# Two leftover transposes move into unused slots of the probability turns, with blocks 1 and 2 of q exchanged and a new turn order

## The chip, the core and the metric

The kernel runs on one core of a Trainium2 chip. The metric is device time in microseconds (us) for one execution. Engines: TensorE (PE in the profile; its weight loads are PEld), VectorE (DVE), ScalarE (ACT), GpSimd (POOL) and SyncE (SP, which here only issues DMAs). Each engine works through its own instructions in order and waits on semaphores for the others.

## The reference

Blocked causal attention over 8 batches of 8 heads with 576 positions of 64 values, and then a mixture of 8 experts over the 4608 tokens, each expert taking at most `capacity` = 80 of them:

```python
scores = scale * q @ k.T                       # per batch and head
mask = (pos[:, None] // 64) >= (pos[None, :] // 64)   # by blocks of 64
attn = softmax(where(mask, scores, -1e9))      # sum + 1e-9 below
x = (attn @ v)                                 # tokens x 512
...
expert = argmax(x @ w_gate); gate = softmax(x @ w_gate)[expert]
out[top 80 tokens of e] = gate * (relu(x @ w1[e]) @ w2[e])   # others 0
```

A position sees all positions of its own block and of the blocks before it. There are 9 blocks, so block 0 of q sees one block of k and block 8 sees nine.

## The kernel before

Two heads of a batch make a pair; there are 32 pairs, four to a batch. Attention is a loop over turns, one for each pair, and in a turn each engine works on several pairs at once. The table `TURN` sets the order: each entry names how many pairs ahead or behind of the current one it works on, and what it does, and every engine takes its instructions in the order of the table. `FIRST` and `LAST` are the tables of the turn ahead of the loop and of the last pair; `TURN` runs for 31 turns.

**Scores.** `prep` transposes q and k of a pair (`T0` and `T1`, on VectorE) and scales q (on POOL, into `qt`). `scores` multiplies them in three groups, each with two PSUM banks (one for each head): group 2 (banks 4, 5) holds the tile "56" (blocks 5 and 6 of q on 128 partitions, 448 columns of k) and "08" (block 0 against block 0 of k, block 8 against block 8); group 1 (banks 2, 3) holds "78" with 512 columns; group 3 (banks 6, 7) holds "34" with 320 columns and "12" with 192. `mask` adds a product of two constants that pushes the masked block down. `max` takes the row maximum on VectorE, `merge` joins the two parts of block 8 and block 0, and `soft` is the exponential on ScalarE, which writes the probabilities to `Pt` and their sums.

**Turning.** The probabilities have q on partitions, and the product with v needs k there. `back` transposes them on TensorE, 64 rows by 128 columns at a time: bank pair A for "78" (banks 6, 7), B for "56" (banks 2, 3), C for "34", half of "08" and part of "12" (banks 0, 1), 16 transposes each, and L (bank 0 again) for what is left, block 8's own block and the third block of "12", 4 transposes. `take` copies a bank from PSUM to `PT`: B0 by VectorE, the others by ScalarE (`TAKE`), L with 256 columns and the others with 512. The last slot of each head in B's first bank turns only zeros, because block 5 of q sees six blocks of k, three column tiles, and has nothing in the fourth.

**Values.** `values` multiplies `PT` with v: 14 products, with long runs of neighbouring blocks as one product, into bank 1 (blocks 1 to 8 of q) and a piece of bank 0 (block 0). The last 64 rows of v (`vt`) stand on partitions 0 to 63, with zeros below. `take` V0 (ScalarE) and V1 (VectorE) copy the result to `xT` in the next turn; `flip` transposes it for storing.

**The small steps.** An entry "t" of the table runs one step of the gate's work of a finished batch on VectorE (`recip`, `products`, `shift`, `first_of`, `weight`, `placed`), "pe" its products on TensorE (`logits` in one turn, `logits2` in the next), "ta" its exponential on ScalarE. A batch's steps are spread over four turns.

After attention the kernel picks 80 tokens for each expert and runs the experts' products, bound by TensorE to the end.

## Time and profile before

| | |
|---|---|
| median of 3 runs | 415.36 us (415.18 to 415.41) |
| profiled execution | 412.34 us, span from the first to the last instruction 410.6 us |
| busy in the span | PE 384.8, PEld 243.8, DVE 282.0, ACT 301.3, POOL 125.5 us |
| granted TensorE clock | 0.987 of full speed in the mean |

Attention takes the span's first 290 us or so, the choice of tokens some 18 us, the experts the rest. A busy PE is not PE at its peak: a record begins when an instruction begins to read and ends when its last result is out, so records overlap, and the distance from one start to the next tells what an instruction costs. The same holds for ACT and DVE, to a smaller degree.

### The profile page before, as it was taken

The page shows a single profiled execution, that of the slowest core. Times are in us where ns is not written, and L with a number is a line of the kernel's source. Part 1 is how long each engine was busy: PE and PEld are TensorE (multiplying, and loading weights), DVE is VectorE, ACT ScalarE, POOL GpSimd, SP SyncE. Part 2 cuts the span into 40 slices and gives each one's busy share as a digit, 9 for nine tenths or more (in the row PEclk, how much of TensorE's full clock was granted, in tenths as well). Part 3 has the DMA queues.
Part 4 walks back from the last instruction along what each step waited for, and adds up shares of the span by engine and source line. Part 5 has one row for each costly group of instructions (what it writes and reads, how often), then busy time and mean ns, then how long its engine had stood idle before and what let it go on. Part 6 is the DMA issues. An engine that isn't in the chain of part 4 may idle for free. (4 is left out here: it accounts for less than half of the span.)

```text
span 410.6 us, 13923 instructions
## 1 busy us (share of the span) xinstructions
PE 384.8 (94%) x5383; PEld 243.8 (59%) x5383; DVE 282.0 (69%) x790; ACT 301.3 (73%) x952; POOL 125.5 (31%) x221
## 2 busy tenths in 40 slices
PE   5889999999999999999999999999899999999970
PEld 3556666666666666566666656665578845667530
DVE  5868788997999899899889989998844400100010
ACT  1889999999999999999999999998121222333240
POOL 6324333433335234244433532300147000000010
PEclk9999999999999999999999999999998999999996
DMA  9979999999999999799999899997659999999100
GB/s 125 136 129 200 154 196 129 211 202 160 175 192 172 147 184 169 123 172 190 149 172 182 139 138 288 379 352 210 223 121 270 367 397 398 397 398 378 51 18 20
DMA packets 199287, 84.31 MB, mean 205 GB/s; under 512 B 163677, under 2 KB 182109, under 8 KB 199216
## 3 DMA queue, kind: packets, MB, share of 16 engines
q1 hardware_dynamic: 190320, 65.79, 72.7%
q0 software_dynamic: 6528, 17.28, 15.8%
q8 instruction: 44, 0.72, 0.8%
q10 hardware_dynamic: 2368, 0.30, 0.6%
q14 instruction: 27, 0.22, 0.2%
HBM read 63.21 MB, written 20.33 MB: 203 GB/s over the span
## 5 line engine op out<-in xcount | busy, mean ns | idle before, releaser
L569 ACT ACTIVATE P<-bank,negm 128x192 f32<-128x192 f32 (+2 forms) x320 | 163.1, 597 | 6.8 <-DVE negm L558 5.9
L537 PE MATMUL bank<-T,qt 64*128 64x320 f32 (+3 forms) x512 | 105.0, 502 | 2.0 <-DVE sameE L284 0.6
L558 DVE TENSOR_REDUCE negm<-bank 128x1 f32<-128x192 f32 (+1 forms) x192 | 87.6, 472 | 16.0 <-PE bank L534 15.9
L627 ACT COPY PT<-bank 128x512 f32<-128x512 f32 (+1 forms) x190 | 91.2, 599 | 6.4 <-PE bank L596 6.3
L616 PE MATMUL bank<-PT,vn 128*64 128x384 f32 (+5 forms) x768 | 93.8, 384 | 0.9 <-ACT PT L627 0.9
L569 ACT ACTIVATION_READ_ACCUMULATOR P<-bank,negm 128x1 f32 x320 | 90.6, 286 | 0.0
L596 PEld LDWEIGHTS bank<-ident,P 64*128 64x128 f32 x1664 | 62.7, 138 | 23.7 <-ACT PT L627 18.5
L596 PE MATMUL bank<-ident,P 64*128 64x64 f32 x1664 | 70.5, 226 | 1.7 <-DVE xT L627 0.9
L616 PEld LDWEIGHTS bank<-PT,vn 128*64 128x64 f32 x768 | 47.6, 137 | 40.8 <-issue 31.2
L512 POOL TENSOR_SCALAR qt<-T 128x576 f32<-128x576 f32 x32 | 21.2, 662 | 147.2 <-DVE raw L558 144.7
L537 PEld LDWEIGHTS bank<-T,qt 64*128 64x128 f32 x512 | 43.5, 186 | 16.9 <-issue 4.5
L507 DVE STREAM_TRANSPOSE T<-ld 128x576 f32<-128x576 f32 x64 | 49.1, 768 | 3.2 <-DMA ld<-in_q_dram 3.2
L558 DVE TENSOR_REDUCE raw<-bank 128x1 f32<-128x64 f32 (+1 forms) x128 | 48.7, 437 | 1.6 <-PE bank L537 1.6
L500 POOL DMA_DIRECT2D vn<-in_v_dram x58 | 45.9, 795 | 1.8 <-PE bank L548 0.9
L1001 PE MATMUL ps<-xsT,w 128*64 128x80 f32 x1024 | 40.8, 239 | 1.3 <-issue 1.3
L1001 PEld LDWEIGHTS ps<-xsT,w 128*64 128x64 f32 x1024 | 38.4, 142 | 5.0 <-issue 4.2
L1055 DVE SCALAR_TENSOR_TENSOR y<-av,comb,yt 80x512 f32<-80x512 f32 x7 | 5.2, 746 | 51.6 <-ACT yt L1054 51.6
L1051 PE MATMUL av<-w,hT 128*32 128x512 f32 (+1 forms) x280 | 37.5, 594 | 0.0
L1054 ACT ACTIVATE yt<-ps,gfar 32x512 f32<-32x512 f32 (+1 forms) x18 | 11.4, 635 | 30.1 <-PE ps L1051 30.0
L1060 POOL DMA_INDIRECT out_dram<-y,si x8 | 7.4, 926 | 76.4 <-DVE y L1055 76.4
L1051 PE MATMUL ps<-w,hT 128*32 128x512 f32 (+1 forms) x72 | 29.1, 547 | 0.0
L1021 ACT ACTIVATE hT<-ps 128x320 f32<-128x320 f32 x16 | 7.0, 438 | 26.2 <-PE ps L1001 26.2
(173 smaller groups left out, 373.2 us busy)
## 6 DMA issues: line engine op xcount, KB each, us to landing
w<-in_moe_w_dram SPq DMA_DIRECT2D x13, 2048.0 KB, 20.2
ld<-in_q_dram SPq DMA_DIRECT2D x128, 72.0 KB, 4.1
xs<-Y SPq DMA_DIRECT2D x32, 288.0 KB, 5.4
out_dram<-zero SPq DMA_DIRECT2D x18, 512.0 KB, 6.8
ld<-in_k_dram SPq DMA_DIRECT2D x124, 72.0 KB, 4.0
vn<-in_v_dram POOLq DMA_DIRECT2D x58, 128.0 KB, 4.2
w<-in_moe_w_dram POOLq DMA_DIRECT2D x8, 512.0 KB, 6.4
w<-in_moe_w_dram POOLq DMA_DIRECT2D x8, 256.0 KB, 6.2
```

What stands on the lines that cost most here:

```text
L500: eng.dma_start(self.vn[:, h], v[b, h0 + h, 0:512].rearrange("(j p) d -> p j d", p=P))
L507: nc.vector.transpose(t, self.nat[x].rearrange("p g d -> p (g d)"))
L512: nc.gpsimd.tensor_scalar(q_, t, scalar1=SCALE, scalar2=1.0, op0=ALU.mult, op1=ALU.mult)
L537: nc.tensor.matmul(s[h][:, c:c + n], lhsT=q_[:, P * t - BLK:P * t + BLK], rhs=k_[:, 0:n], start=(c == 0), stop=(g == "1"))
L558: nc.vector.tensor_reduce(to[:, b, h:h + 1], self.s[g][h][:, c:c + n], axis=AX.X, op=ALU.max, negate=True)
L569: nc.scalar.activation(Pt[self.i % 2][u][:, h, 0:n], self.s[g][h][:, c:c + n], AF.Exp, bias=self.negm[:, t, h:h + 1], scale=1.0, accum_out ...
L596: nc.tensor.transpose(pt[c][:, n_ * BLK:(n_ + 1) * BLK], row[u][r, h, P * j:P * (j + 1)], ident[r, r])
L616: nc.tensor.matmul(to, lhsT=self.vt[:, h, :] if j == 4 else self.vn[:, h, j, :], rhs=self.PT[:, h, row, b0:b1].rearrange("p b r -> p (b r) ...
L627: (nc.scalar.copy if (eng or TAKE[x]) == "a" else nc.vector.tensor_copy)(*self.out.pop(x))
L1001: yield nc.tensor.matmul(dst(b)[64 * c:64 * (c + 1)], lhsT=w_[:, a, col:col + 64], rhs=x_[:, a], start=(a == 0), stop=(a == n - 1))
L1051: last = nc.tensor.matmul(to[col:col + s1 - s0, c0:c1], lhsT=hT[:, a, s0:s1], rhs=w_[:, a, c0:c1], start=(a == ends[0]), stop=(a == ends[1 ...
L1054: nc.scalar.mul(t[s0:s1, c0:c1], rest[g][FAR:FAR + s1 - s0, c0:c1], gfar[FAR:FAR + s1 - s0, g, e:e + 1])
```

## The change

Bank L goes. Block 0's probabilities are written to columns 64 to 127 of a wider, cleared tile "08" (`SKIP`), and their turn takes the slot of B in which block 5's fourth tile turned zeros (columns 64 to 191, so that block 0 of k lands on partitions 0 to 63). Block 8's own block is turned with a slot of C, from the same cleared tile, so that it lands on partitions 64 to 127, and block 4's last 64 columns are turned over the upper half of the same slot. Blocks 1 and 2 of q change places in `qt`, so that "12" needs its third block in the first half of the partitions, and `mask` and its constants follow. `PT` has 6 slots for a row instead of 8. `values` goes through these slots with 28 products instead of 14, with block 8 in a bank of its own (bank 0) and the last two steps of half a slot each. `recip` has two more operations, because the sums of blocks 1 and 2 have changed halves. `TAKE` gives B0 to ScalarE and B1 to VectorE. The turn's order is new.

```diff
-TAKE = {"A0": "a", "A1": "a", "B0": "v", "B1": "a", "C0": "a", "C1": "a", "L": "a", "V0": "a", "V1": "v"}
+TAKE = {"A0": "a", "A1": "a", "B0": "a", "B1": "v", "C0": "a", "C1": "a", "V0": "a", "V1": "v"}
...
-WIDE = {"78": 512, "56": 512, "34": 384, "12": 256, "08": P}
+WIDE = {"78": 512, "56": 512, "34": 320, "12": 256, "08": 3 * BLK}
+SKIP = {"08": BLK}
...
     def recip(self):
...
+            for to, of in ((slice(0, BLK), slice(BLK, P)), (slice(BLK, P), slice(0, BLK))):
+                yield nc.vector.tensor_scalar(self.rs[to, 1], s_[of, 1], scalar1=1e-9, scalar2=None, op0=ALU.add)
...
-            eng.dma_start(self.vt[0:BLK], v[b, h0:h0 + 2, 512:576].rearrange("h p d -> p h d"))
+            eng.dma_start(self.vt[BLK:P], v[b, h0:h0 + 2, 512:576].rearrange("h p d -> p h d"))
...
-            nc.gpsimd.tensor_scalar(q_, t, scalar1=SCALE, scalar2=1.0, op0=ALU.mult, op1=ALU.mult)
+            tb, qb = (y.rearrange("p (b r) -> p b r", r=BLK) for y in (t, q_))
+            for to, of in ((slice(1, 3), slice(2, 0, -1)), (slice(0, 1), slice(0, 1)), (slice(3, 9), slice(3, 9))):
+                nc.gpsimd.tensor_scalar(qb[:, to], tb[:, of], scalar1=SCALE, scalar2=1.0, op0=ALU.mult, op1=ALU.mult)
...
+                todo_ = [(c, 4 * h + n_, h, *of) for h in range(2) for c, n_, of in (
+                    (0, 0, whole("34", 0)), (1, 0, whole("34", 0)), (0, 1, whole("34", 1)), (1, 1, whole("34", 1)),
+                    (0, 2, whole("12", 1)), (1, 2, whole("08", 0)), (0, 3, whole("12", 0)), (1, 2, ("34", slice(4 * BLK, 5 * BLK))),
+                    (1, 3, whole("12", 0)))]
...
-            steps = [(0, 0, 2, 8, 2), (0, 3, 2, 4, 0), (1, 1, 1, 8, 1), (2, 2, 3, 8, 3), (3, 3, 5, 8, 5), (4, 1, 0, 1, 7),
-                     (0, 2, 2, 3, None)]
+            steps = [(0, 0, 0, 5, 3), (0, 0, 5, 6, 8), (0, 3, 1, 2, 1), (0, 3, 0, 1, 2), (0, 3, 2, 3, 0), (1, 1, 0, 5, 3),
+                     (1, 1, 5, 6, 8), (1, 2, 0, 1, 2), (2, 2, 2, 5, 5), (2, 2, 5, 6, 8), (3, 3, 3, 5, 6), (3, 3, 5, 6, 8)]
...
+            for h in range(2):
+                r = slice(h * D, (h + 1) * D)
+                nc.tensor.matmul(av[r, 4 * BLK:5 * BLK], lhsT=self.vn[0:BLK, h, 2, :], rhs=self.PT[0:BLK, h, 2, 1],
+                                 start=False, stop=True)
+                nc.tensor.matmul(a8[r], lhsT=self.vt[BLK:P, h, :], rhs=self.PT[BLK:P, h, 2, 1], start=False, stop=True)
```

In the new table a turn begins with the `T0` transpose for the pair after next, then V1, group 2, five "t", B, the deferred soft (12,1), V0, B0, A, A0, C, then the other copies and the maxima; the second `prep` stands between the maxima of group 2 and group 1, `merge` behind the softs of "56", and the softs of "08" ahead of those of "78". `flip` takes the pair one back instead of two back, so a batch's small steps begin one turn earlier.

ScalarE in one turn before, from V0's copy (`xT`) to the first soft of the next pair:

```order
L627 COPY xT_2781<-bank1_3067 128x512
L627 COPY PT_3135<-bank3_3137 128x8x64
L627 COPY PT_3135<-bank7_3156 128x8x64
L627 COPY PT_3135<-bank0_3174 128x8x64
L627 COPY PT_3135<-bank6_3155 128x8x64
L627 COPY PT_3135<-bank1_3175 128x8x64
L627 COPY PT_3135<-bank0_3203 128x2x128
L569 ACTIVATE P56_0_129,sums_2783<-bank4_3122,negm_3113 128x448
```

ScalarE at the same place now:

```order
L635 COPY xT_3006<-bank1_3862 128x512
L635 COPY PT_3928<-bank2_3929 128x8x64
L635 COPY PT_3928<-bank6_3950 128x8x64
L635 COPY PT_3928<-bank7_3951 128x8x64
L635 COPY PT_3928<-bank0_3969 128x8x64
L635 COPY PT_3928<-bank1_3970 128x8x64
L572 ACTIVATE P56_1_138,sums_3732<-bank4_3915,negm_3907 128x448
```

Six copies in the order B1, A1, C0, A0, C1, L have become five, in the order B0, A0, A1, C0, C1.

TensorE before, from group 1 (bank2, bank3) over L's four transposes (`P08`, `P12`) to group 3 (bank6, bank7):

```order
L537 MATMUL bank2_3199<-T1_3088,qt0_138 128x512
L537 MATMUL bank3_3200<-T1_3088,qt0_138 128x512
L596 MATMUL bank0_3203<-ident_79,P08_1_137 128x64
L596 MATMUL bank0_3203<-ident_79,P12_1_136 128x64
L596 MATMUL bank0_3203<-ident_79,P08_1_137 128x64
L596 MATMUL bank0_3203<-ident_79,P12_1_136 128x64
L537 MATMUL bank6_3210<-T1_3088,qt0_138 128x320
L537 MATMUL bank7_3211<-T1_3088,qt0_138 128x320
```

TensorE now, the end of values (`vn` and `vt1` hold v; each row is one product for one head, or as many as its x tells):

```order
L619 MATMUL bank1_3494<-PT_3392,vn_2990 64x320 x2
L619 MATMUL bank0_3495<-PT_3392,vn_2990 64x64 x2
L619 MATMUL bank1_3494<-PT_3392,vn_2990 64x64 x2
L619 MATMUL bank1_3494<-PT_3392,vn_2990 64x192 x2
L619 MATMUL bank0_3495<-PT_3392,vn_2990 64x64 x2
L619 MATMUL bank1_3494<-PT_3392,vn_2990 64x128 x2
L619 MATMUL bank0_3495<-PT_3392,vn_2990 64x64 x2
L624 MATMUL bank1_3494<-PT_3392,vn_2990 64x64
L626 MATMUL bank0_3495<-PT_3392,vt1_145 64x64
L624 MATMUL bank1_3494<-PT_3392,vn_2990 64x64
L626 MATMUL bank0_3495<-PT_3392,vt1_145 64x64
```

Group 3 now follows group 1 directly, and values goes between bank 0 and bank 1, in many products of 64 columns.

VectorE now, at the head of a turn with the steps of `recip`: `T0` is the moved transpose, `xT` V1's copy, `negm<-bank4` the first maximum, `PT` the copy B1:

```order
L508 STREAM_TRANSPOSE T0_3359<-ld0_2805 128x576
L635 COPY xT_3006<-bank0_3305 128x64
L459 COPY Wt_178<-bank0_3305 128x5x4x2
L358 TENSOR_TENSOR sums_2284<-sums_2284,sums8_2285 64x8
L359 COPY sums_2284<-sums8_2285 64x8
L360 TENSOR_SCALAR rs_2287<-sums_2284 128x40
L362 TENSOR_SCALAR rs_2287<-sums_2284 64x8
L561 TENSOR_REDUCE negm_3357<-bank4_3377 128x1
L635 COPY PT_3392<-bank3_3394 128x8x64
L561 TENSOR_REDUCE raw_3358<-bank4_3377 128x1
```

Before, the transpose of T0 stood behind the copy and the second maximum of "56"; now it is the first row of the turn.

## Rows read from the trace of the kernel before

**Rows 1.** Busy time by stage: stretch, its length, then each engine's us (instructions).

```profile
106.00:140.00 34.00, 33.91 (x474) 21.25 (x470) 30.89 (x82) 33.25 (x111) 13.24 (x21) 1.00 1.02 176
```

**Rows 2.** Timeline of TensorE, one turn: start, length, engine, line, operation, tiles, count.

```profile
213.38 0.97 PE L537 MATMUL bank<-T,qt 64*128 64x448 f32 x4
214.28 0.22 PE L548 MATMUL bank<-mneg,mrow 64*64 64x64 bf16 x2
...
214.57 1.71 PE L596 MATMUL bank<-ident,P 64*128 64x64 f32 x48
216.23 1.13 PE L537 MATMUL bank<-T,qt 64*128 64x512 f32 x4
217.20 0.41 PE L596 MATMUL bank<-ident,P 64*128 64x64 f32 x4
217.51 1.14 PE L537 MATMUL bank<-T,qt 64*128 64x320 f32 x8
218.48 0.22 PE L548 MATMUL bank<-mneg,mrow 64*128 64x128 bf16 x2
218.63 2.70 PE L616 MATMUL bank<-PT,vn 128*64 128x384 f32 x20
221.16 0.28 PE L616 MATMUL bank<-PT,vt 128*64 128x64 f32 x4
221.27 0.29 PE L616 MATMUL bank<-PT,vn 128*64 128x64 f32 x4
221.49 1.02 PE L537 MATMUL bank<-T,qt 64*128 64x448 f32 x4
```

**Rows 3.** Timeline of TensorE, groups 2, 1 and 3 in the neighbouring turns.

```profile
204.85 1.02 PE L537 MATMUL bank<-T,qt 64*128 64x448 f32 x4
...
207.64 1.08 PE L537 MATMUL bank<-T,qt 64*128 64x512 f32 x4
...
209.04 1.14 PE L537 MATMUL bank<-T,qt 64*128 64x320 f32 x8
...
224.29 1.13 PE L537 MATMUL bank<-T,qt 64*128 64x512 f32 x4
...
225.73 1.13 PE L537 MATMUL bank<-T,qt 64*128 64x320 f32 x8
```

**Rows 4.** Timeline of ScalarE: L's copy and what follows it, then all six copies.

```profile
199.72 0.48 ACT L627 COPY PT<-bank 128x256 f32<-128x256 f32 x1
...
199.98 0.75 ACT L569 ACTIVATE P<-bank,negm 128x448 f32<-128x448 f32 x1
...
215.40 2.82 ACT L627 COPY PT<-bank 128x512 f32<-128x512 f32 x6 [0.19 <-PE bank L596]
...
218.06 0.69 ACT L569 ACTIVATE P<-bank,negm 128x448 f32<-128x448 f32 x1
```

**Rows 5.** Waits from 100 to 300: who waited for whom, us, times, longest.

```profile
PEld bank L596 <- ACT PT L627: 12.8, 21, 0.7
...
PEld bank L537 <- ACT PT L627: 2.7, 16, 0.2
```

**Rows 6.** Timeline of VectorE: first maxima, products, copy B0 and a T0 transpose.

```profile
206.22 0.63 DVE L558 TENSOR_REDUCE negm<-bank 128x1 f32<-128x448 f32 x1 [1.03 <-PE bank L534]
...
213.57 0.69 DVE L403 TENSOR_TENSOR prod<-bank,rs 128x80 f32<-128x80 f32 x4 [0.48 <-PE bank L397]
...
214.97 0.61 DVE L558 TENSOR_REDUCE negm<-bank 128x1 f32<-128x448 f32 x1
215.50 0.68 DVE L627 COPY PT<-bank 128x512 f32<-128x512 f32 x1
...
216.84 0.77 DVE L507 STREAM_TRANSPOSE T<-ld 128x576 f32<-128x576 f32 x1
```

**Rows 7.** Timeline of POOL: the scaling of q.

```profile
217.77 0.66 POOL L512 TENSOR_SCALAR qt<-T 128x576 f32<-128x576 f32 x1 [5.36 <-DVE raw L558]
```

**Rows 8.** Timeline of TensorE's weight loads: the four for vt.

```profile
221.00 0.31 PEld L616 LDWEIGHTS bank<-PT,vt 128*64 128x64 f32 x4
```

More of the change, by code (lines that the diff above doesn't have):

```diff
@@ L41 @@
     (1, "begin"),
+    (2, "prep", 0),
     (0, "pe"),
+    (-1, "take", "V1"),
+    (1, "scores", "2"),
     (0, "t"),
@@ L46 @@
     (0, "t"),
-    (-1, "take", "V1"),
     (0, "t"),
-    (1, "scores", "2"),
-    (0, "soft", "34", 1),
+    (0, "back", "B"),
+    (0, "soft", "12", 1),
     (-1, "take", "V0"),
+    (0, "take", "B0"),
+    (0, "back", "A"),
+    (0, "take", "A0"),
+    (0, "back", "C"),
     (1, "max", "56", 0),
-    (0, "back", "B"),
+    (0, "take", "A1"),
     (0, "take", "B1"),
-    (0, "back", "A"),
-    (0, "take", "B0"),
-    (0, "back", "C"),
-    (0, "take", "A1"),
+    (0, "ta"),
     (0, "take", "C0"),
-    (0, "take", "A0"),
-    (0, "t"),
+    (0, "take", "C1"),
+    (1, "max", "08", 0),
     (1, "max", "56", 1),
-    (0, "t"),
-    (2, "prep", 0),
+    (2, "prep", 1),
     (1, "scores", "1"),
-    (0, "back", "L"),
-    (0, "take", "C1"),
-    (0, "ta"),
-    (1, "max", "08", 0),
-    (1, "scores", "3"),
     (1, "max", "78", 0),
@@ L73 @@
     (1, "max", "78", 1),
-    (1, "merge"),
-    (0, "take", "L"),
-    (0, "values"),
+    (0, "t"),
     (1, "soft", "56", 0),
     (1, "soft", "56", 1),
+    (1, "merge"),
+    (1, "soft", "08", 0),
+    (1, "soft", "08", 1),
+    (1, "scores", "3"),
+    (1, "max", "12", 0),
+    (1, "max", "34", 0),
+    (1, "max", "12", 1),
+    (1, "max", "34", 1),
+    (-1, "flip"),
     (1, "soft", "78", 0),
-    (1, "soft", "08", 0),
     (1, "soft", "78", 1),
-    (1, "max", "12", 0),
-    (2, "prep", 1),
-    (1, "max", "34", 0),
-    (-2, "flip"),
-    (1, "max", "12", 1),
-    (1, "soft", "08", 1),
-    (1, "max", "34", 1),
+    (0, "t"),
     (1, "soft", "12", 0),
     (1, "soft", "34", 0),
-    (1, "soft", "12", 1),
+    (1, "soft", "34", 1),
+    (0, "values"),
     (3, "load_v"),
@@ L122 @@
     (1, "soft", "34", 0),
-    (1, "soft", "12", 1),
+    (1, "soft", "34", 1),
     (3, "load_v"),
@@ L131 @@
     (-1, "take", "V1", "v"),
-    (0, "soft", "34", 1),
+    (0, "soft", "12", 1),
     (-1, "take", "V0", "v"),
@@ L143 @@
     (0, "take", "A0", "v"),
-    (0, "back", "L"),
     (0, "take", "C0", "a"),
     (0, "take", "C1", "v"),
-    (0, "take", "L", "a"),
     (0, "values"),
@@ L209, in tile_attn_moe @@
     for h in range(2):
-        nc.vector.memset(mrow[h * D:h * D + 1, 0:BLK], 1.0)
-        nc.vector.memset(mneg[h * D:h * D + 1], -1e30)
+        for i in range(2):
+            r = h * D + 32 * i
+            nc.vector.memset(mrow[r:r + 1, i * BLK:(i + 1) * BLK], 1.0)
+            nc.vector.memset(mneg[r:r + 1, i], -1e30)
     wgd = const.tile([P, NP, 32], F32, name="wgd")
@@ L579, in back @@
             if not hasattr(self, "PT"):
[L580 removed]
+                self.PT = big.tile([P, 2, 4, 6, BLK], F32, name="PT")
             pt = banks(x, self.where)
             halves = [slice(c * BLK, (c + 1) * BLK) for c in range(2)]
[L583 to L593 removed]
@@ L594, in back, with whole @@
-            for c, n_, u, h, j in todo_:
-                r = halves[c]
-                nc.tensor.transpose(pt[c][:, n_ * BLK:(n_ + 1) * BLK], row[u][r, h, P * j:P * (j + 1)], ident[r, r])
-            if x == "L":
-                self.out["L"] = (self.PT[:, :, 1, 0:2], pt[1][:, 0:4 * BLK].rearrange("p (h s r) -> p h s r", h=2, s=2))
-            else:
-                for c in range(2):
-                    self.out[f"{x}{c}"] = (self.PT[:, :, :, {"A": 6, "B": 4, "C": 2}[x] + c],
-                                           pt[c].rearrange("p (h j r) -> p h j r", h=2, j=4))
+            def whole(u, j):
+                return u, slice(P * j, P * (j + 1))
@@ L604, in values @@
+            for c, n_, h, u, cols in todo_:
+                r = halves[c]
+                nc.tensor.transpose(pt[c][0:cols.stop - cols.start, n_ * BLK:(n_ + 1) * BLK], row[u][r, h, cols], ident[r, r])
+            for c in range(2):
+                self.out[f"{x}{c}"] = (self.PT[:, :, :, {"A": 4, "B": 2, "C": 0}[x] + c],
+                                       pt[c].rearrange("p (h j r) -> p h j r", h=2, j=4))
         def values(self):
-            (av,), a0 = banks("av", self.where), self.last[:, 4 * BLK:5 * BLK]
+            (av,), (self.last,) = banks("av", self.where), banks("L", self.where)
@@ L607, in values @@
+            a8 = self.last[:, 4 * BLK:5 * BLK]
             if turns:
```

34 lines of the change are left out of this document (13 added, 21 removed).

## The prediction

> **What bounds the kernel now.** I read the busy time by stage first, then TensorE's own timeline of one turn, then the same places of its neighbours, then ScalarE and VectorE beside it. In the attention stage no engine has much room: of 34 us, PE is recorded busy 33.91, ACT 33.25 and DVE 30.89 [rows 1]. PE's figure counts overlapping instructions, so its starts have to be read. In the turn from 213.38 to 221.49 [rows 2] they follow one another with hardly a hole: scores of group 2, 48 transposes, group 1, four more transposes (bank L), group 3, values. The one place where PE is held up is around bank L. The four transposes may not start before ScalarE has emptied bank 0 (copy C0), and group 3 not before it has emptied bank 6 (copy A0). In the waits these are the two rows in which weight loads stand for ScalarE's copies: 12.8 us in 21 turns and 2.7 us in 16 [rows 5]; most of the first is covered by group 1, which is still streaming. ScalarE waits in this turn only for the first transposes, 0.19 us before its six copies [rows 4]. So PE and ScalarE form one loop: transposes, four copies, group 3, values, group 2, transposes. VectorE has slack in it: in one turn it waits 1.03 us for the scores, in the next 0.48 us for another product of PE [rows 6].
>
> **What bank L costs PE.** From the start of group 1 to the start of group 3, three turns in a row spend 1.40 (207.64 to 209.04), 1.28 (216.23 to 217.51) and 1.44 us (224.29 to 225.73) [rows 2, 3], 1.37 in the mean. Afterwards nothing stands between the two groups. Group 1 streams four times 512 columns, 2048 in all; group 3 streams four times 320 and four times 192, also 2048, and takes 0.97 us, from 217.51 to the mask at 218.48 [rows 2]. So 1.37 becomes 0.97: **-0.40 us a turn**. This holds if both groups find their banks empty, which is weighed under ScalarE.
>
> **Transposes.** 52 become 50: L's four go, C has 18 instead of 16, A and B keep 16 (block 0 of q takes a slot of B that turned zeros). The two more in C cost 2 x 35 ns, from 48 in 1.66 us between 214.57 and 216.23 [rows 2]: **+0.07**.
>
> **Values.** 14 products become 28, over the same 25 blocks of 64 columns for each head. Each fp32 product is two instructions, so 28 instructions become 56, and 40 of them have only 64 columns. A long run puts 20 instructions with 5888 columns into 2.53 us (218.63 to 221.16), 0.43 ns a column, so 64 columns should take 27.5 ns; the four with `vt` take 0.11 us (221.16 to 221.27), 28 ns each [rows 2]. By that row the split is nearly free, which is the lower end. At the upper end the short instructions go at the transposes' 35 ns: 40 x 7 ns = 0.28. The last four products use half of the contraction rows, a form that values did not have. The nearest change of form stands in group 2: 1792 columns at 0.43 ns are 0.77 us, but the mask follows after 0.90 (213.38 to 214.28 [rows 2]); so 0 to 0.13 for that. I take 0.06 for each, nearer to the rows of the same line: **+0.12**, with ends at 0 and 0.41.
>
> **ScalarE.** The copy of L goes: 0.26 us from its start at 199.72 to the next activation at 199.98 [rows 4]; its record of 0.48 overlaps with that. PE's sum, -0.40 + 0.07 + 0.12 = **-0.21 us** of some 8.5 (204.85 to 213.38 [rows 2, 3]), shortens the turn by 2.5%, and ScalarE by 3%: it stays some 2 to 3% under PE, and PE leads, but not by much. Its new order is V0, B0, A0, A1, C0, C1. The six copies take 2.66 us now (215.40 to 218.06 [rows 4]), of which L 0.26, so 0.48 for each of the others. Counted from the start of group 2, B's transposes start at 1.19 (213.38 to 214.57) and end at 1.75, so B0 can start near 1.95 and A1 ends near 3.4. PE, with 50 transposes and group 1, is at group 3 at 1.19 + 1.75 + 0.97 = 3.9. C1 ends near 4.4, and values begin at 5.0. So neither place should wait for ScalarE, with some 0.5 us to spare.
>
> **VectorE.** A T0 transpose of 0.77 us [rows 6] moves to the head of the turn, ahead of V1, up to five small steps and the first maximum; B1 behind them is now VectorE's copy, and group 1's second half needs its bank. In a turn like the one from 204.85 the move fills the 1.03 us for which VectorE waits for the scores anyway [rows 6]. The turn with the products has less of a hole: the 0.48 us ahead of them, and the maximum starts at 214.97, 1.59 us after group 2, against 206.22 - 204.85 = 1.37 [rows 2, 3, 6]. Of 0.77 us 0.48 fit in. I charge between 0 and 0.3 us in one turn of four, half of it: 7 x 0.15 = **+1.0 us** in the run. Without the cover of these waits it is the second rival. Two more small operations for a batch are nothing against 9% of idle time.
>
> **POOL.** One scaling becomes three: 0.66 us now, after 5.36 us of waiting [rows 7]; three would be 0.66 to 2.0. Behind them in POOL's queue stand the loads of v for three pairs on, and the scaled q is read a turn later. Hidden; without that cover up to 1.3 us would hold up group 2.
>
> **Edits that cost nothing.** Soft (12,1) is deferred where (34,1) was, a shorter activation ahead of V0. Flip and the gate's steps come a pair earlier: the same operations, in VectorE's idle time. Cleared buffers are written ahead of the loop; loads of v keep their size and queue; SP keeps its order but for the store of each batch, which goes behind one more turn's q and k, and those are loaded five pairs ahead. The experts' stage is the same and begins when attention ends.
>
> **The sum.** TURN runs 31 times: 31 x -0.21 = -6.5, and +1.0: **-5.5 us**. The profiled execution's own 412.34 us (span 410.6) would be 406.8; the median of the runs shown, 415.36, stands 3.0 above it, and the forecast is made against that: **409.9 us**. With the ends of the unknown terms: -0.40 + 0.07 + 0 = -0.33 a turn, -10.2 in all and 405.1; -0.40 + 0.07 + 0.41 = +0.08 a turn, +2.5 and VectorE's 2 more: 419.9.
>
> **Rivals.**
> *The hand-over eats it.* PE's gain is there, but ScalarE ends its deferred soft or V0 late, and the transposes of A and C, which need banks 7, 0 and 1, wait. ScalarE's margin is only some 0.2 us a turn, so that much is enough. For it: ScalarE's 98% [rows 1]. Against it: L's copy frees 0.26. With half of PE's 0.21 lost: 415.36 - 3.3 + 1 = 413.1; with all of it, the same time as before. Chance 0.17, two thirds of it still faster.
> *VectorE's head holds up group 1.* Place: B1, behind T0, V1, five steps and the first maximum. Today's copy in its place starts at 215.50 and takes 0.68, to 216.18 [rows 6]; group 1's second half starts some 0.5 us later, at 216.7. Price: 0.77 less 0.5 is 0.27 on PE, and as much again where the late merge delays ScalarE: 0.27 to 0.54 a turn. It decides from 0.21 on, if in every turn; at 0.4 it gives 31 x 0.19 = +5.9 and 421, **slower**. Against it: 1.03 us of idle time in a turn that has no products. Chance 0.08.
> *Short products go at the pace of their weight loads.* Four loads for `vt` stand in 0.31 us, 78 ns each at most [rows 8]. If the matmuls had to keep to that, 40 x 50 ns = 2.0 us a turn, some 56 us more in all, 471. It decides at 28 + 210/40 = 33 ns each. Against it: `vt` itself ran at 28 ns with these loads [rows 2]. Chance 0.05. The Trainium skill (TensorE: Matmul & The Clock Gate, section LDWEIGHTS) gives a load as its columns divided by 1.2, in ns, which is 53 ns for 64 columns; by that, as an estimate, the turn would grow by some 0.8 us and the time be near 440. The 28 ns row speaks against it, if only for a short run.
> *A larger gain.* The split is free and nothing waits: 404 to 406.5. Chance 0.13.
> *It does not do what it says.* L's copy and transposes are gone in every turn of the new order, so this has no chance of its own.
>
> **How the numbers follow.** Forecast, 406.5 to 412.5: 0.57. Larger gain 0.13, hand-over 0.17, VectorE 0.08, loads 0.05. 0.2% (0.8 us) is about what a measurement of this kernel can tell from no change. Faster: 0.57 + 0.13 + 0.11 = 0.81, less 0.04 of the forecast for a wait that I did not see, 0.77. Same: 0.06 of the hand-over and 0.03 of that, 0.09. Slower: 0.13 and 0.01, 0.14. The range from 404.0 to 416.0 leaves out the slower cases and the far end of the larger gain.
>
> **What would show it.** In the trace after: group 1 to group 3 at 0.97 us in every turn; no transpose or score that waits for ScalarE's copies; values near 2.98 us instead of 2.86 (218.63 to 221.49 [rows 2]); ScalarE at 95 to 98% of the stage. What would make it wrong: a first maximum that starts over 1.6 us after group 2 in more than one turn of four, values above 3.2 us, or transposes of A or C that wait for V0 or the soft of 12.

## The result and the profile after

The changed kernel takes **419.62 us** (median of 4 runs, 417.16 to 420.97) against 415.38 us: a ratio of 1.0093, 95% interval 1.0068 to 1.0117. It is slower by 1%, 9.7 us above the forecast and outside its range. The profiled execution took 417.16 us, with a span of 415.4 us against 410.6 us; the two profiles therefore differ by 4.8 us, the medians by 4.2. Some executions of these kernels take over 1.5% longer than the fastest of their kind; the ratios and intervals below leave them out, the medians don't.

A steady turn first. Windows by stage in the form of [rows 1], and one turn of TensorE in the form of [rows 2]:

```profile
174.00:208.00 34.00, 33.94 (x582) 25.11 (x579) 32.08 (x87) 32.99 (x109) 15.13 (x30) 1.00 0.91 162
```

```profile
187.15 1.02 PE L540 MATMUL bank<-T,qt 64*128 64x448 f32 x4
...
188.39 1.90 PE L601 MATMUL bank<-ident,P 64*128 64x64 f32 x48
190.07 0.67 PE L540 MATMUL bank<-T,qt 64*128 64x512 f32 x1
...
192.17 0.35 PE L453 MATMUL bank<-sp,sameR 128*32 128x40 f32 x16
192.45 2.77 PE L619 MATMUL bank<-PT,vn 128*64 128x320 f32 x48
...
195.43 1.18 PE L384 MATMUL bank<-xT,wgd 128*32 128x288 f32 x16
```

This is the turn in which a batch's `sameR` products stand ahead of values. The turn of the same kind before, from group 1 to values:

```profile
198.05 1.13 PE L537 MATMUL bank<-T,qt 64*128 64x512 f32 x4
...
200.89 2.70 PE L616 MATMUL bank<-PT,vn 128*64 128x384 f32 x20
```

From the start of group 1 to the start of values it takes 2.38 us now (190.07 to 192.45), against 2.84 (198.05 to 200.89). The four kinds of turn of a batch differ; in the mean of the four this distance fell from 2.58 to 2.22 us, by 0.36. Of that, group 1 to group 3 alone fell from 1.39 to 0.93, and group 3 to values grew by 0.1. The transposes take 1.68 us (188.39 to 190.07), values 2.98 (192.45 to 195.43). ScalarE is busy 97% of the stretch. In the waits from 100 to 280 us the row of transposes that stand for ScalarE's copies [rows 5] is gone. Values and the scores still wait for copies, 0.2 us at a time and in 11 turns each; a third row is new:

```profile
PEld bank L619 <- ACT PT L635: 2.3, 11, 0.2
...
PEld bank L540 <- ACT PT L635: 2.2, 11, 0.2
...
DVE T L508 <- DMA ld<-in_q_dram: 1.4, 1, 1.4
```

VectorE's first maximum of two turns, and the start of group 2 in the same turns:

```profile
204.97 1.03 PE L540 MATMUL bank<-T,qt 64*128 64x448 f32 x4
...
213.05 1.02 PE L540 MATMUL bank<-T,qt 64*128 64x448 f32 x4
```

```profile
206.83 0.62 DVE L561 TENSOR_REDUCE negm<-bank 128x1 f32<-128x448 f32 x1
...
214.86 0.61 DVE L561 TENSOR_REDUCE negm<-bank 128x1 f32<-128x448 f32 x1
```

The distances are 1.86 and 1.81 us; in the other two turns of a batch it is 1.36.

Now the length of a batch, four turns, from one product with the gate's weights (`logits`) to the next. Before, and then after:

```profile
203.75 1.18 PE L383 MATMUL bank<-xT,wgd 128*32 128x288 f32 x16
238.31 1.18 PE L383 MATMUL bank<-xT,wgd 128*32 128x288 f32 x16
289.02 1.19 PE L383 MATMUL bank<-xT,wgd 128*32 128x288 f32 x16 [0.32 <-DVE xT L627]
```

```profile
89.81 1.18 PE L384 MATMUL bank<-xT,wgd 128*32 128x288 f32 x16
125.04 1.18 PE L384 MATMUL bank<-xT,wgd 128*32 128x288 f32 x16
161.50 1.18 PE L384 MATMUL bank<-xT,wgd 128*32 128x288 f32 x16
...
287.69 1.72 PE L384 MATMUL bank<-xT,wgd 128*32 128x288 f32 x16 [0.37 <-DVE xT L635]
```

Before, a batch takes 34.56 us (203.75 to 238.31). After, the undisturbed ones take 33.92 (as from 161.50 to 195.43): 0.64 us less. But two in the middle take 35.23 and 36.46 us (89.81 to 125.04 to 161.50), together 3.85 us more than two undisturbed ones. So the last batch's logits come at 287.69 in place of 289.02, only 1.33 us earlier.

**Where the middle lost it.** VectorE after, ahead of the transposes of pair 11 and pair 16, with TensorE and the windows behind the second:

```profile
91.67 0.78 DVE L508 STREAM_TRANSPOSE T<-ld 128x576 f32<-128x576 f32 x1 [2.39 <-DMA ld<-in_q_dram]
...
135.74 0.78 DVE L508 STREAM_TRANSPOSE T<-ld 128x576 f32<-128x576 f32 x1 [1.36 <-DMA ld<-in_q_dram]
```

```profile
137.07 3.09 PE L601 MATMUL bank<-ident,P 64*128 64x64 f32 x48 [1.18 <-DVE prod L404]
139.88 1.09 PE L540 MATMUL bank<-T,qt 64*128 64x512 f32 x1
```

```profile
135.60:137.30 1.70, 0.52 (x12) 0.29 (x11) 1.52 (x7) 0.93 (x4) 0.60 (x3) 1.00 0.56 91
137.30:140.80 3.50, 3.45 (x52) 3.27 (x53) 3.23 (x6) 2.12 (x5) 2.62 (x5) 0.51 0.95 179
```

T0 now heads VectorE's turn, and there VectorE stood still 2.39 and 1.36 us for a load of q. Behind T0 wait V1, the products and the maxima. Two other kernels with the same middle (a_noclr and a_tail below) stall at the same two pairs. TensorE waited 1.18 us for the products, because B's banks hold the logits until VectorE has read them; then its granted clock fell to 0.51 in the mean, the lower of its two levels (1.2 GHz), and the transposes took 2.81 us (137.07 to 139.88) in place of the 1.54 of an undisturbed turn of this kind. So 1.36 us on VectorE made a turn of 10.8 us (134.58 to 145.37) out of one of 8.1.

Why was q late? SyncE's queue, before and after, around the loads of pair 11:

```profile
69.94 2.06 SPq L491 DMA_DIRECT2D ld<-in_q_dram  x4
...
74.51 0.44 SPq L370 DMA_DIRECT2D xs<-rs  x1
```

```profile
75.02 1.31 SPq L371 DMA_DIRECT2D xs<-rs  x1
...
81.14 7.30 SPq L492 DMA_DIRECT2D ld<-in_q_dram  x4
```

Before, pair 11's q was issued by 72.00, ahead of the first store (`xs`), and transposed at 94.67, 22.7 us later. After, the first store stands ahead of it, its four issues took 7.30 us in place of 2.06, and they ended at 88.44, 3.2 us ahead of T0. I call this distance the **lead** of a q load. From pair 11 on it is 18 to 28 us before and 3 to 12 us after. SyncE was already some 5 us behind: the loads of pair 10 ended at 69.85 before and at 74.93 after. The order moved for this one store only: the first store stands behind the loads of 11 pairs in place of 12, the later ones behind 16, 20, 24 and 28 in both kernels.

**Where the hand-over lost it.** SyncE from the clears on, before and after, and then GpSimd's first gather and TensorE ahead of the first expert:

```profile
248.64 22.92 SPq L228 DMA_DIRECT2D out_dram<-zero  x16
...
279.58 3.02 SPq L228 DMA_DIRECT2D out_dram<-zero  x2
288.78 0.39 SPq L326 DMA_DIRECT2D w<-in_moe_w_dram  x1
...
295.88 3.82 SPq L373 DMA_DIRECT2D xs<-Y  x4
```

```profile
258.85 21.32 SPq L227 DMA_DIRECT2D out_dram<-zero  x16
...
286.98 2.93 SPq L227 DMA_DIRECT2D out_dram<-zero  x2
290.29 0.96 SPq L325 DMA_DIRECT2D w<-in_moe_w_dram  x1
...
295.00 6.97 SPq L374 DMA_DIRECT2D xs<-Y  x4
```

```profile
304.58 1.14 POOL L896 DMA_INDIRECT xg<-xs,gi  x1 [4.43 <-ACT occ L943]
```

```profile
307.82 1.15 POOL L902 DMA_INDIRECT xg<-xs,gi  x1 [8.54 <-PE ps L645]
```

```profile
302.26 4.80 PE L645 MATMUL ps<-identr 128*128 128x512 f32 x20
311.34 1.00 PE L1016 MATMUL pm<-ident,xn 80*128 80x80 f32 x4 [4.27 <-DVE xn L996]
```

The gather needs two things, the indices (`gi`) and the stored tokens. VectorE's indices, before and after:

```profile
303.32 0.17 DVE L886 TENSOR_REDUCE gi<-ps 80x8 int32<-80x16 f32 x1 [0.38 <-PE ps L882]
```

```profile
302.45 0.17 DVE L892 TENSOR_REDUCE gi<-ps 80x8 int32<-80x16 f32 x1 [0.38 <-PE ps L888]
```

The trace's records have the last store landing at 303.59 before, 0.1 us behind the indices, and at 306.83 after, 4.2 us behind them; in both the gather starts 1.0 us after the landing. The row of the gather after names TensorE's fillers, which end at about the same time.

The last batch's store is issued at nearly the same time, but with the clears 10 us later, two of them go out just ahead of it, together with 2 MB of weights that stand there before as well. From its issue to the gather it takes 12.8 us (295.00 to 307.82) in place of 8.7. From 275 to 290 us the DMA engines are busy 0.93 and move 311 GB/s, against 0.61 and 170. TensorE's filler products (`identr`) end at about 307; it stands 4.27 us, and from 310 to 320 its granted clock is 0.66 in the mean, against 0.83:

```profile
275.00:290.00 15.00, 13.05 (x223) 9.54 (x219) 11.18 (x36) 10.14 (x32) 1.01 (x2) 1.00 0.93 311
310.00:320.00 10.00, 6.88 (x81) 5.74 (x83) 3.30 (x19) 0.89 (x3) 7.79 (x15) 0.66 0.80 236
```

```profile
275.00:290.00 15.00, 13.75 (x210) 9.29 (x210) 12.29 (x37) 10.85 (x35) 1.00 (x2) 1.00 0.61 170
310.00:320.00 10.00, 10.00 (x185) 9.11 (x187) 3.72 (x21) 1.73 (x4) 5.86 (x12) 0.83 1.03 300
```

The spans' 4.8 us add up: last logits -1.33; from there to the gather 20.13 in place of 15.56, +4.57; from the gather to the end 107.58 in place of 106.02, +1.56. The last term may not be the change's: from the first gather to the last scatter of results, where the profile of before has 95.5 us, two kernels made from it below (b_noclr, b_cover) have 97.5 and 97.9.

### The profile page after: what moved, and what is told of

The parts are those of the page before. It is cut to its first block, busy times and chain, and to the rows that moved or that the text cites. A ratio compares the mean times of both kernels' runs of the same rounds, so it can differ in the third digit from the quotient of the medians.

```text
span 415.4 us, 15645 instructions
## 1 busy us (share of the span) xinstructions
PE 383.1 (92%) x6215; PEld 272.2 (66%) x6215; DVE 285.4 (69%) x810; ACT 293.7 (71%) x920; POOL 134.8 (32%) x279
## 3 DMA queue, kind: packets, MB, share of 16 engines
q0 software_dynamic: 6528, 17.28, 15.7%
## 5 line engine op out<-in xcount | busy, mean ns | idle before, releaser
L572 ACT ACTIVATE P<-bank,negm 128x448 f32<-128x448 f32 (+4 forms) x320 | 163.9, 564 | 11.8 <-DVE negm L561 6.3
L540 PE MATMUL bank<-T,qt 64*128 64x192 f32 (+3 forms) x512 | 102.6, 491 | 1.3 <-DVE sameR L284 0.9
L619 PE MATMUL bank<-PT,vn 128*64 128x64 f32 (+3 forms) x1536 | 88.7, 272 | 1.0 <-ACT dl L418 1.0
L635 ACT COPY PT<-bank 128x512 f32<-128x512 f32 x158 | 82.6, 641 | 7.2 <-PE bank L601 6.6
L619 PEld LDWEIGHTS bank<-PT,vn 128*64 128x64 f32 x1536 | 67.2, 137 | 23.9 <-ACT PT L635 3.6
L572 ACT ACTIVATION_READ_ACCUMULATOR P<-bank,negm 128x1 f32 x320 | 80.7, 252 | 0.0
L515 POOL TENSOR_SCALAR qt<-T 128x128 f32<-128x128 f32 (+2 forms) x96 | 31.3, 345 | 143.7 <-DVE xT L635 73.6
L540 PEld LDWEIGHTS bank<-T,qt 64*128 64x128 f32 x512 | 59.6, 188 | 19.1 <-issue 5.1
L601 PE MATMUL bank<-ident,P 64*128 64x64 f32 (+1 forms) x1600 | 63.3, 228 | 3.4 <-DVE xT L635 1.2
L601 PEld LDWEIGHTS bank<-ident,P 64*128 64x128 f32 (+1 forms) x1600 | 57.5, 140 | 7.0 <-DVE xT L635 1.5
L1057 PE MATMUL av<-w,hT 128*32 128x512 f32 (+1 forms) x280 | 37.5, 594 | 0.0
L1057 PE MATMUL ps<-w,hT 128*32 128x512 f32 (+1 forms) x72 | 29.1, 548 | 0.0
```

The costliest lines, as they stand in the source:

```text
L515: nc.gpsimd.tensor_scalar(qb[:, to], tb[:, of], scalar1=SCALE, scalar2=1.0, op0=ALU.mult, op1=ALU.mult)
L540: nc.tensor.matmul(s[h][:, c:c + n], lhsT=q_[:, P * t - BLK:P * t + BLK], rhs=k_[:, 0:n], start=(c == 0), stop=(g == "1"))
L572: nc.scalar.activation(Pt[self.i % 2][u][:, h, c1:c1 + n], self.s[g][h][:, c:c + n], AF.Exp, bias=self.negm[:, t, h:h + 1], scale=1.0, acc ...
L601: nc.tensor.transpose(pt[c][0:cols.stop - cols.start, n_ * BLK:(n_ + 1) * BLK], row[u][r, h, cols], ident[r, r])
L619: nc.tensor.matmul(a8[r] if c0 == 8 else av[r, BLK * c0:BLK * (c0 + b1 - b0)], lhsT=self.vn[:, h, j, :], rhs=self.PT[:, h, row, b0:b1].rea ...
L635: (nc.scalar.copy if (eng or TAKE[x]) == "a" else nc.vector.tensor_copy)(*self.out.pop(x))
```

## The experiments

Two theories to begin with. **Head**: T0 at VectorE's head turns late loads into stalls. **Queue**: SyncE's queue trails, which makes both the stalls and the late hand-over. The rival, **Turn**: the new order itself costs more than it saves. "A" below is the changed kernel, "B" the kernel before. Ratios stand against runs of the kernel before on the same chip, whose medians are 415.5 to 416.1 us, so ratios are the better comparison.

| kernel | median us | ratio (95%) | undisturbed batch us | VectorE's waits on q after the start | lead of q, pairs 11, 16 | last logits to gather |
|---|---|---|---|---|---|---|
| before | 415.38 | 1 | 34.56 | none | 22.7, 18.4 | 15.6 |
| changed | 419.62 | 1.0093 (1.0068 to 1.0117) | 33.92 | 2.39, 1.36, 0.26 | 3.2, 5.0 | 20.1 |
| a_t0 | 419.67 | 1.0077 (1.0054 to 1.0101) | 34.95 | none | 13.9, 15.6 | 16.0 |
| a_early | 415.77 | 0.999 (0.996 to 1.002) | 33.92 | none | 12.3, 13.8 | 19.7 |
| a_t0_early | 419.95 | 1.0101 (1.0061 to 1.0141) | 34.92 | none | 21.0, 29.0 | 16.0 |
| a_noclr | 413.42 | 0.992 (0.9886 to 0.9954) | 33.90 | 3.7 in two | 4.7, 5.5 | 16.2 |
| b_noclr | 415.49 | 0.9993 (0.9975 to 1.001) | 34.54 | none | 21.7, 13.2 | 15.8 |
| a_t0late | 429.47 | 1.0315 (1.0269 to 1.0361) | 36.00 | none | 20.4, 25.2 | 16.0 |
| b_t0 | 418.55 | 1.0056 (1.003 to 1.0081) | 34.73 | none | 15.4, 8.8 | 15.6 |
| a_t0t1 | 417.42 | 1.0002 (0.9967 to 1.0038) | 34.01 | none | 7.4, 6.6 | 22.3 |
| a_store0 | 418.51 | 1.0069 (1.0037 to 1.01) | 33.91 | none | 16.0, 10.0 | 21.9 |
| a_tail | 415.95 | 0.9991 (0.9961 to 1.0021) | 33.90 | 2.7 in two | 3.7, 5.3 | 18.4 |
| a_mend | 415.01 | 0.996 (0.9926 to 0.9994) | 33.91 | none | 12.7, 12.4 | 18.3 |
| b_mend | 417.45 | 1.0028 (1.001 to 1.0046) | 34.56 | none | 29.1, 23.3 | 15.7 |
| a_cover | 414.07 | **0.9952 (0.9928 to 0.9976)** | 33.89 | none | 12.3, 16.7 | 17.5 |
| b_cover | 415.83 | 0.9985 (0.9966 to 1.0005) | 34.56 | none | 27.7, 25.0 | 15.6 |
| a_cover_store0 | 415.96 | 1.0006 (0.997 to 1.0042) | 33.89 | 0.36 | 18.9, 12.3 | 25.0 |
| a_cover_t0t1 | 415.07 | 0.9967 (0.9932 to 1.0001) | 34.00 | none | 16.6, 21.3 | 20.9 |

The last four columns come from each kernel's profiled execution.

**T0 moved back, in A (a_t0).**

```diff
     (1, "begin"),
-    (2, "prep", 0),
...
     (1, "max", "56", 1),
+    (2, "prep", 0),
     (2, "prep", 1),
```

> The changed kernel with one line moved back: the q transpose T0 of the pair two turns ahead stands behind the maximum of rows 5 and 6 again, not at the head of VectorE's turn. Theory Head (VectorE's queue, stopped at its head by a q load that lands late, costs the 2.4 and 1.4 us waits of the middle of attention and the clock that falls after them, about 3.8 us together): about 416 us, no wait of VectorE on a q load after the first turns, and the batches of the middle as long as the later ones, 33.9 us. Theory Queue (SyncE's queue of loads trails by some 10 us, which makes the stalls of the middle and also the late end at the hand-over): also about 416 us, since the wait has 3 to 4 us more cover, but the q loads are still issued only 5 to 12 us ahead of their use and the gather still starts 3 us later than in the kernel before. Rival Turn (the new order itself costs more than it saves): 419 to 420, nothing moves.

The stalls went and the time did not, so both theories missed and the number is Turn's: every batch took 34.95 us. The gather was punctual too, 16.0 us after the logits, which Queue had not expected: with q asked for later in longer turns, the leads grew to 13 to 28 us. Both transposes in a row on VectorE, with the maxima and `merge` (L565) behind them, in one steady turn, and then waits from 150 to 280 us:

```profile
192.34 1.43 DVE L508 STREAM_TRANSPOSE T<-ld 128x576 f32<-128x576 f32 x2
193.70 1.38 DVE L561 TENSOR_REDUCE raw<-bank 128x1 f32<-128x512 f32 x3
195.11 0.22 DVE L565 SCALAR_TENSOR_TENSOR negm<-raw,lower 128x4 f32<-128x4 f32 x1
```

```profile
PEld bank L398 <- ACT P L572: 3.7, 8, 0.5
ACT P L572 <- DVE raw L561: 2.9, 7, 0.4
```

The two put off the maxima and `merge`, which ScalarE's softs need, and TensorE waits for the softs; the changed kernel has 1.2 and 0.4 us in these rows from 100 to 280 us. A turn grew by 0.26 us. So the move took the stalls away and put a new wait in their place.

**The experts' first weights later, in A (a_early).**

```diff
-            if i >= 2 and i % 3:
+            if i >= 10 and i % 3:
                 next(early, None)
```

> The changed kernel with the 16 early loads of the experts' first weights begun at turn 10 in place of turn 2; T0 stays at the head of VectorE's turn. Theory Queue: the loads of the first 90 us have the DMA engines more to themselves, SyncE gets ahead, the q loads of pairs 11 and 16 are issued 15 us or more ahead of their use as in the kernel before, both stalls vanish and the clears come earlier: 412 to 415 us. Theory Head alone with the queue as an accident: the stalls only move to other turns, 418 to 420. Rival Turn: 419 to 420.

T0 is still at the head, yet no stall: the 3.85 us of the middle are gone, and some 4 in the time (ratio 1.0093 to 0.999), though the top of the expected range was missed by 0.8. This settles the middle against Turn: with the loads in time, the batches of the new order keep their 33.92 us. These weights are issued by GpSimd, not by SyncE, so what SyncE's loads gained is room among the transfers and not an earlier place in its queue. The hand-over stayed 4 us late, although the clears began 7 us earlier (251.5).

**Both (a_t0_early).** The two edits above.

> Both edits: T0 behind the maximum of rows 5 and 6, and the experts' first weights from turn 10 on. If Queue holds, T0's place is worth little once the loads are early: within 1 us of the kernel that has the later weights alone, 411 to 415. If Head holds and Queue does not: as with T0 moved alone, about 416. Rival Turn: 419 to 420.

Neither: leads of 21 to 32 us, no stall, and still 34.92 us a batch. That a_t0 lost its gain to its own turn, and not to loads, follows from this run.

**Without the clears, in A and in B (a_noclr, b_noclr).**

```diff
-            if 0 <= i < nz:
+            if 0 <= i < 0:
                 eng.dma_start(ov[i], zero.rearrange("p (r d) -> p r d", r=2))
```

> The changed kernel without the 18 clears of the output (512 KB each, left out altogether, so the rows of tokens that no expert takes are not set to zero). It prices the tail: theory Queue says that the store of batch 6, the last weights and the last batch's store then go out with nothing ahead of them, the gather starts when its indices are there (about 302.5 us) in place of 307.8, and the time falls by 4 to 6 us, to about 414 to 415, with the stalls of the middle unchanged. If the tail hangs on something else (indices, weights), it falls by under 1.5 us.

> The kernel before without the 18 clears of the output (left out altogether), the control to the changed kernel without them, which fell by 6 us. Theory Queue: the clears are over before its last store, so the gather starts where it did, 15.6 us after the last logits, and the time falls by under 2 us. If it falls by 4 us or more, the clears cost both kernels alike and the tail's loss is not the change's.

A fell by 6 to 7 us, with its stalls still there (3.7 us), and its gather came 16.2 us after the logits. The profiles show 4 us of that, ahead of the gather; where the rest comes from is not shown. B did not move. The clears cost nothing where they are over in time, and 4 us ahead of the gather alone where they run into the last store.

**T0 at other places (a_t0late, b_t0, a_t0t1).** At the end of A's turn; at the head in B; and in A with both transposes where B has them:

```diff
     (1, "begin"),
-    (2, "prep", 0),
...
     (1, "max", "34", 1),
+    (2, "prep", 0),
     (-1, "flip"),
```

```diff
     (1, "begin"),
+    (2, "prep", 0),
     (0, "pe"),
...
     (0, "t"),
-    (2, "prep", 0),
     (1, "scores", "1"),
```

```diff
     (1, "begin"),
-    (2, "prep", 0),
...
     (1, "max", "56", 1),
-    (2, "prep", 1),
+    (2, "prep", 0),
...
     (1, "max", "12", 0),
+    (2, "prep", 1),
```

> The changed kernel with T0 of the pair two turns ahead at the end of VectorE's share of the turn, behind the last maximum of rows 3 and 4 and ahead of the flip: some 6 us later than at the head, but out of the way of the maxima that the scores wait for (at its old place, behind the maximum of rows 5 and 6, it made every batch 34.95 us long in place of 33.92). Theory Place (the batch's length hangs on what stands ahead of the maxima of rows 7 and 8 on VectorE, the stalls of the middle on how late in the turn the q load is asked for): batches of 33.9 us throughout, no stall in the middle, the tail as in the changed kernel, 415 to 416.5. If the scores of the next turn then wait for q's scaling, 34.5 us or more a batch: 418 or more. Theory Queue says nothing else than the tail: the gather still 3 us or more later than attention's end allows.

> The kernel before with T0's transpose alone moved to the head of VectorE's turn. It asks whether the steady gain of the change (34.56 to 33.92 us a batch) comes from T0's place or from the transposes and banks. If from T0's place: batches of about 34 us here, and with q asked for some 4 us earlier the 20 us of lead keep the stalls away: 412 to 414 us. If from the transposes (the forecast's reading: L's 0.40 us a turn less what the values and the other transposes add): batches of 34.5 us or more, 415 to 417.

> The changed kernel with both transposes of the pair two turns ahead where the kernel before has them: T0 behind the maximum of rows 5 and 6, T1 behind the first maximum of rows 1 and 2. If the mid-turn loss of T0 moved alone (34.95 us a batch) came from two transposes in a row ahead of the maxima of rows 7 and 8: 33.9 to 34.2 us a batch, no stalls, 415 to 416.5. If T0 has to stand at the head for the steady gain: 34.6 us or more a batch, 418 to 420.

At the turn's end it is too late: TensorE waits for q's scaling in each turn, and a batch takes 36.00 us:

```profile
189.43 1.02 PE L540 MATMUL bank<-T,qt 64*128 64x448 f32 x4 [0.96 <-POOL qt L515]
```

In B the head is worth nothing: 34.73 us a batch, over 2 us more in all by the ratio, more than either reading had expected, and leads of 8 to 16 us around the middle. In A, with both transposes at B's places, a batch takes 34.01. So the steady gain does not come from T0's place, and needs T0 at the head only as long as T1 stands right behind T0's old place. What the transposes and banks bring, and what the rest of the new order, no run separates. That run's time shows the hand-over again: its clears began at 259.4, and the gather came 22.3 us after the logits.

**The first store behind 12 pairs, in A (a_store0).**

```diff
-        fill(bt.recip, None, (bt.store,))
-        fill(bt.products, "l2")
+        fill(bt.recip, None, (bt.store,) if bt.b else ())
+        fill(bt.products, "l2", () if bt.b else (bt.store,))
```

> The changed kernel with the first batch's store behind the loads of 12 pairs on SyncE, as in the kernel before, in place of 11; nothing else moves. Theory Store (the store put ahead of pair 11's loads takes their lead): pair 11's q is issued some 10 us ahead of its use in place of 3.2, the 2.4 us stall there goes, and 1 to 3 us of time with it: 416.5 to 418.5; the tail stays. Theory Queue without it (general contention): the stall comes back at pair 12 or 13 and the time stays at 419 to 420.

In the profile, Store is borne out: pair 11's lead is 16.0 us and no stall is left, in a run of 414.87 us. But the other runs of the kernel lie at 418 to 421, and the median hardly differs from the changed kernel's. The store's place explains pair 11 in the profile; what it is worth in the time stays open.

**SyncE's order at the end, in A (a_tail); with the weights from turn 8 on as well, in A and in B (a_mend, b_mend).**

```diff
-            for _ in range(4 if i >= n - 5 else 0):
+            for _ in range(5 if i >= n - 5 else 0):
...
-        weights(1)
         lt = bt.logits_of()
...
         bt.store()
+        weights(1)
```

In a_mend and b_mend, besides:

```diff
-            if i >= 2 and i % 3:
+            if i >= 8 and i % 5:
```

> The changed kernel with SyncE's order at the end of attention changed: all 18 clears ahead of the store of batch 6 (five a turn in place of four), and the 2 MB weight load that stood ahead of the last batch's store behind it. Theory Queue: the last store has the DMA engines nearly to itself, as without the clears, and the time falls by 2 to 5 us, to 415 to 417.5; the stalls of the middle stay. If the clears cost by their bytes alone, wherever they stand, the time falls by under 1.5 us.

> The changed kernel with SyncE's order at the end as in the run before (18 clears ahead of the store of batch 6, the weight load behind the last store) and the 16 early weight loads between turns 8 and 27 in place of 2 and 25. Theory Queue: the stalls of the middle go (3.9 us, as measured with the later weights alone) and the gather starts some 16 us after the last batch's logits, as in the kernel before: 410 to 412.5 us. Rival Turn: no better than the later weights alone, 415 to 416.

> The kernel before with the same two edits of the loads, as a control. Its q loads are issued some 20 us ahead of their use and its last store finds the DMA engines idle, so theory Queue says that neither edit has anything to win there: within 1 us of the kernel before. If it falls by 3 us or more, the edits are worth the same everywhere and say nothing on the change.

The tail alone gave some 4 us in the ratio, as expected, with all the bytes still there: the place of the clears and the weights counts. Its profile, a run of 417.01 us, shows only part of it, 18.4 us to the gather in place of 20.1. Together with the later weights it did not reach 412.5, and B got slower by 1.4. In all three, weights that are issued only at 297 to 300 us seem to put off the first expert: 36.1 to 37.5 us from the gather to the first scatter of results, against 32.5 before and up to 35.5 in the other kernels.

**The later weights and the clears, the last weight load left in place (a_cover, b_cover).**

```diff
-            if i >= 2 and i % 3:
+            if i >= 10 and i % 3:
...
-            for _ in range(4 if i >= n - 5 else 0):
+            for _ in range(5 if i >= n - 5 else 0):
```

> The changed kernel with two edits of the loads and no other: the 16 early weight loads from turn 10 on, and all 18 clears ahead of the store of batch 6 (five a turn). The weight load at the end keeps its place ahead of the last store, since moving it back cost the first expert some 2 us in the two runs that did. Theory Queue: no stall in the middle, the gather some 16 to 17 us after the last batch's logits: 411 to 414 us, faster than the kernel before. If the tail's loss is the clears' bytes and not their place, 415 to 416 as with the later weights alone.

> The kernel before with the same two edits, as a control. Theory Queue: nothing to win, since its loads come 20 us early and its last store finds the DMA engines idle: within 1 us of the kernel before, batches of 34.56 us, the gather 15.6 us after the last logits. Rival: the two edits are an improvement of any kernel, and it falls as far as the changed one does (4 us or more).

A is now faster than the kernel before by 0.5%. Its median, 414.07, is at the top of the expected range; its fastest runs, 410.6, come near the forecast. B gains nothing that the interval tells from zero: the two edits pay only where the queue trails. In A's profile the clears end at 276.5, and the gather starts with the store's landing, which here is named outright:

```profile
250.77 25.76 SPq L227 DMA_DIRECT2D out_dram<-zero  x18
...
291.20 4.71 SPq L374 DMA_DIRECT2D xs<-Y  x4
```

```profile
301.39 1.12 POOL L902 DMA_INDIRECT xg<-xs,gi  x1 [5.92 <-DMA xs<-Y]
```

**On top of that, the edit of a_store0 or that of a_t0t1 (a_cover_store0, a_cover_t0t1).**

> The two edits of the loads that beat both kernels (weights from turn 10, clears ahead of batch 6's store), and the first store behind 12 pairs of loads. No stall is left to save there, so the time stays within 1 us of those two edits alone, 413 to 415; if the larger lead brings the clears and the last store forward, up to 1.5 us less.

> The two edits of the loads, with T0 and T1 where the kernel before has them. If the steady gain keeps without T0 at the head, as good as the two edits alone or up to 1.5 us better (more lead, earlier clears): 412 to 414.5. If T0 has to stand at the head: 416 to 418.

Neither adds anything: 1.0006 (0.997 to 1.0042), and 0.9967 (0.9932 to 1.0001) with 415.07 us. The first one lost a_cover's gain. In its profile the clears began at 260.4, 10 us later than in a_cover, with an order on SyncE that differs in one store near 75 us, and the gather came 25.0 us after the logits, the longest of all, although the clears ended at 284.3, ahead of the changed kernel's 289.9. How far SyncE trails late in attention is therefore not set by its order alone.

## Why the prediction was wrong

**Right, and nearly to the size:** the bank that went. Group 1 to group 3 fell by 0.46 us a turn and group 1 to values by 0.36, where 0.40 was forecast for L's place; the transposes took 1.61 us in the mean of four turns against 1.59 (forecast +0.07), values 2.98 (forecast 2.98), ScalarE 97% (forecast 95 to 98), and no transpose waits for its copies. A batch lost 0.64 us; four times -0.21 and 0.15 for VectorE would be -0.69. That the sums agree so well is in part luck: 0.27 us a batch were lost where nothing was charged, behind values in the turn with the gate's transposes (3.22 us to 3.61, of which the split is 0.12). ScalarE's margin at the start of values was forecast as 0.5 us; values wait for its copies in half of the turns, 0.2 us each. Three scalings of q on POOL stayed hidden: but for single waits of up to 0.5 us, TensorE waits for q only in a_t0late, where T0 was moved to the end.

**VectorE's head, half right.** The first maximum starts 1.36 us after group 2 in two turns of a batch, 1.86 in the turn with the products and 1.81 in the next. More than one turn in four over 1.6 us was named as a sign that the forecast is wrong; it came, and by itself it cost nothing that the turns show: these two take 8.09 and 8.02 us, against 8.11 and 8.22 before. So the sign was badly chosen, and the +1.0 us charged for this place does not show. But the step priced T0 as 0.77 us of work. It is also an instruction that waits for a DMA, and at the head of an in-order engine it passes the wait on to all behind it. That was not in the sum: 3.85 us in the profile.

**SP "keeps its order but for the store ... loaded five pairs ahead", at no cost: the step that failed.** Five pairs ahead in the program is no lead in time. Nor does each store go behind one more turn's loads: the first goes behind one pair fewer, the others stay. SyncE issued without a pause of more than 0.6 us between 60 and 250 us in both kernels; four loads of q took about 2 us at the least and up to 7.30. A batch's issues came 33.25 us apart on average after (stores at 119.85 and 252.85, four batches), so batches of 33.92 us give back hardly 0.7 us of lead each. What was lost up to pair 11 was still missing at the clears. The Trainium skill (Perfetto Trace Analysis, section What "DMA-bound" means) names an issuing queue that is solid with DMA slices as one of three ways to be bound by DMA, and says that such a slice is the making of descriptors. The row here is solid; that the same four loads took 2.06 and 7.30 us says that more than their making is in it. The DMA engines behind it were full too: from 60 to 250 us they were busy 0.99 before and 0.92 after ([rows 1] has 1.02). Whether the queue or the engines set the pace, no run separates.

**"The experts' stage is the same and begins when attention ends": failed.** It begins when the indices are there and the last store has landed. With the clears 10 us later the gather came 4.57 us later after the logits. a_noclr and b_noclr show some 4.1 of that to be the clears', and a_tail and a_cover that their place counts; the other 0.4 is the change's own, since A takes 16.0 us even where the store is punctual (a_t0, a_t0_early, a_t0late). In the profiles these two failed steps cost 3.85 and 4.57 us, and 1.56 more were lost behind the gather, part of it, it seems, to a lower granted clock. Together that is 10.0 us, about what lies between the forecast gain of 5.5 and the measured loss of 4.8.

**The rivals.** The slower one forecast 421, close to the result, but for a reason that did not come true: B1 holding up group 1 in every turn. The undisturbed batches show nothing of it; B1 did hold up group 1 in the turn of pair 11's stall, where TensorE's weight loads waited 1.07 us for it. Loads as pace of the short products: values at 2.98 us rule out that rival. The Trainium skill (TensorE: Matmul & The Clock Gate, section LDWEIGHTS) gives 53 ns for a load of 64 columns; the 0.8 us a turn that the forecast estimated from it did not come. The list of what would make the forecast wrong had no entry on a load or a store, and both causes were there.

**Open:** why SyncE's lead differs by up to 10 us between runs of nearly the same order; why a_cover's last store still lands 1.6 us behind its indices (300.40 and 298.81); why the other runs of the changed kernel were 2 to 4 us slower than the profiled one, and how much of that is the stalls and how much the clock after the gather. Its spread, 3.8 us in 4 runs against 0.5 in the 4 before, is no sign by itself: 29 other runs of the kernel before spread over 4.6.

## What to carry to other kernels

An instruction that waits for a DMA is priced by the lead of that load, read as a time between issue and use in the trace, and by all that stands behind it on its engine; moving it 4 us forward spends 4 us of lead, as long as the load isn't issued earlier too. When compute gets faster, ask for each queue of transfers whether it has the time left to follow: this one was solid with issues, and the gain was paid back at the first place where compute had to wait for it. Spread what isn't needed soon (weights, clears) over the stretch where the queue has room, and keep the queue empty ahead of the one store that the next stage waits for. In this case that paid 0.5% against the kernel before, and one small edit more on the same queue lost it again.

## What the runs showed of the hardware

The longer stall of VectorE did less harm than the shorter one: at pair 11 (2.39 us) TensorE itself waited 0.24 us, its granted clock stayed at 1.00 and the batch grew by 1.31 us; at pair 16 (1.36 us) it waited 1.18 us, the clock fell to its lower level while 50 transposes took 2.81 us in place of 1.54, and the batch grew by 2.54. And kernels whose loads stand in nearly the same order (a_cover, a_cover_store0) issued their clears 10 us apart.
